# One row of the up weights in two transfers, and the order of the four matmuls that use it

## The chip, the cores and the metric

The kernel runs on one core of one Trainium2 chip. The metric is device time in microseconds (us): the median of several runs, beside the time of one profiled execution whose trace is read here. The core has TensorE (PE in the profile; PEld is its loading of weights), VectorE (DVE), ScalarE (ACT), GpSimd (POOL) and SyncE (SP), which in this kernel only issues DMA transfers.

## The reference

One layer adds two branches to its input. Inputs and output are bf16.

```
xn  = layernorm(x)                                   # x: 2048 tokens x 512
dt  = exp(log_dt);  L = exp(dt * Lambda)             # 512 complex states
Bu  = xn @ (((L - 1) / Lambda)[:, None] * B).T
h_t = L * h_(t-1) + Bu_t                             # a scan over 2048 tokens
y   = 2 * Re(h @ C.T) + xn * Dskip
f   = (silu(xn @ w_gate) * (xn @ w_up)) @ w_down     # 512 -> 1376 -> 512
out = x + y + f
```

## The kernel before, in words

The 2048 tokens are four chunks (`CW` = 512 tokens) of four tiles of 128 tokens. The instructions of each engine stand in the order in which the Python code emits them; the framework adds the semaphores. Dependences on DMA are kept by transfer: whoever reads a part of a tile waits for the transfers that wrote this part. Hardware-issued transfers take eight landing counters in turn, and an issue whose counter is still taken waits until the transfer eight places before it has landed.

Most of the span is a long sequence of matmuls, chunk after chunk: `bproj_tile` (L387, states of the scan), `gateup_tile` (L462, gate and up products), `out_ffn` (L605) and `out_ssm` (L618, the two parts of the output). VectorE's scans and rotations come between these from a backlog with planned costs (`queue`, `pump`, `need`); the coefficients `CF` of the last matmuls are made there too (L373).

The change lies at the start, where nothing is loaded yet. Chunk 0 is done token-major: a tile of tokens is the stationary side, the weights stream as the moving side, 512 columns at a time. The columns of the gate and up weights are cut into feature groups 0 and 1 (512 columns each) and a rest of 352 (`fgroups`, L89). `wg01` and `wu01` hold groups 0 and 1 of gate and up, 1024 columns (`FE`) in four rows `k`; row `k` has the weights for input features 128k to 128k + 127.

The SP queue issues, in this order: token tile 0 (L123); the four rows of up (L128, through `load_row`, L117), 256 KB each; rows 0 and 1 of gate; token tile 2 (L131); row 2 of gate; token tile 3 (L133); row 3 of gate; the rest columns of gate and up (`w_end`, L113); the tokens of chunk 1 (L141). ScalarE issues token tile 1 (L125), GpSimd three small parameter rows (L140). Later on the SP queue stand transposing transfers: chunk 0's tokens (L258) and the two parts of B (`BT`, L145), which wait for VectorE's work on tiles 2 and 3.

For tiles 0 and 1, TensorE transposes the raw tokens (L231), VectorE subtracts the mean (`centered`, L248, into `CF`, whose memory serves as scratch here) in six steps: tile 0 rows 0 and 1, tile 1 rows 0 and 1, then rows 2 and 3 of each tile in one. TensorE then multiplies row by row, `row_mm(which, k)`, with `which` 0 for up and 1 for gate: for each row four matmuls (L494), two tiles times two feature groups, into four accumulators in PSUM that are complete after row 3. ScalarE takes the up accumulators out (L514), while TensorE goes on with the gate rows, a small transpose of the parameters (L278) and the transposes of token tile 2.

Of the kernel before, what the change touches and what calls it, by code (L numbers as in the profile page):

```python
# [23 lines left out]
def kernel(  # L24
# [17 lines left out]
    nc = tc.nc  # L42
# [31 lines left out]
    def bank(shape=(128, CW), dtype=F32):  # L74
        return psum.tile(list(shape), dtype, name="ps")
# [7 lines left out]
    wu_v = B_w_up.rearrange("(k p) f -> p k f", p=128)  # L83
# [6 lines left out]
    FE = fgroups[-1][0] * 128  # L90
    wg01 = const.tile([128, KD, FE], BF16, name="wg01")
    wu01 = const.tile([128, KD, FE], BF16, name="wu01")
# [23 lines left out]
    def load_row(q, t, view, k):  # L116
        q.dma_start(out=t[:, k, :], in_=view[:, k, 0:FE])  # L117
# [7 lines left out]
    nc.scalar.dma_start(out=xall[:, 1, :], in_=x_v[:, 1, :])  # L125
    nc.scalar.preload_act_table_set("silu_and_others")
    for k in range(KD):
        load_row(nc.sync, wu01, wu_v, k)  # L128
    for k in range(HK):
        load_row(nc.sync, wg01, wg_v, k)  # L130
    nc.sync.dma_start(out=xall[:, 2, :], in_=x_v[:, 2, :])  # L131
# [93 lines left out]
    pair = [[[bank() for _ in range(2)] for _ in range(2)] for _ in range(2)]  # L225
# [260 lines left out]
    def tokens(i, k):  # L486
        if i < SW:
            return xcT[:, k, i * 128:(i + 1) * 128]
        return xnT0[:, k, i, :]

    def sw_mm(ps, groups, gi, i, k0=0, k1=KD):
        a, b = fgroups[gi]
        for k in range(k0, k1):
            nc.tensor.matmul(ps[:, 0:(b - a) * 128], lhsT=tokens(i, k), rhs=groups[gi][:, k, 0:(b - a) * 128],  # L494
                             start=(k == 0), stop=(k == KD - 1))
# [202 lines left out]
    G, U = wg_g, wu_g  # L698
# [14 lines left out]
        centered(i, HK, KD)  # L713

    def row_mm(which, k):
        for i in range(2):
            for gi in range(2):
                sw_mm(pair[which][i][gi], (U, G)[which], gi, i, k, k + 1)

    for k in range(KD):  # L720
        row_mm(0, k)
# [6 lines left out]
    for n in range(2):  # L728
        norm_dve(n)
    row_mm(1, 0)  # L730
    pp = prm_transpose()
    ln_stats(2)
# [6 lines left out]
    for k in range(1, SW):  # L739
        row_mm(1, k)  # L740
# [167 lines left out]
```

## Time and profile before

| | us |
|---|---|
| median of 3 runs | 177.86 |
| the three runs | 177.73, 177.86, 178.3 |
| the profiled execution | 178.45 |
| its span, first to last instruction | 176.2 |
| TensorE busy in the span | 171.9 (98%) |
| VectorE busy | 157.6 (89%) |
| ScalarE busy | 102.7 (58%) |
| GpSimd busy | 28.1 (16%) |

The granted TensorE clock was 1.0 throughout. The profile's rows give starts in us from the start of the span; a matmul's end is modelled, so that two matmuls that follow each other overlap in the rows. A DMA row gives the issuing engine's start and the time of the issue; the time from issue to landing stands in a separate view. "idle before" is the time in which an engine did nothing ahead of an instruction, with what ended it.

### The profile page before, as it was taken

The numbers are of one execution on the slowest core, as the hardware profiler recorded it, in microseconds if no ns is written. First come the engines' busy times: TensorE is split into PE (matmuls) and PEld (weight loads), VectorE is DVE, ScalarE is ACT, GpSimd is POOL, SyncE is SP. The second block draws the span as 40 slices with busy tenths as digits, with TensorE's granted clock in tenths as the row PEclk, the third lists the DMA queues.
The fourth block names the chain that finished last, engine by engine and source line by source line (L and its number), as shares of the span: only waits on it lengthen the run. The fifth ranks groups of instructions, "written<-read, shape, count | busy, mean of one in ns | idle before, by whom it ended". The sixth has DMA issues, their size and how long they took to land.

```text
span 176.2 us, 2377 instructions
## 1 busy us (share of the span) xinstructions
PE 171.9 (98%) x859; PEld 81.9 (46%) x859; DVE 157.6 (89%) x261; ACT 102.7 (58%) x188; POOL 28.1 (16%) x39
## 2 busy tenths in 40 slices
PE   7899999999999999999999999999999999999993
PEld 4344445464444444446444444446444444444543
DVE  3877999999999999999999999999999998699542
ACT  4179599794996685236598661024666653991100
POOL 5244110022000000044300000024100000521700
PEclk9999999999999999999999999999999999999999
DMA  5997949999999300037016000007310000696831
GB/s 169 357 342 147 142 90 208 287 188 297 151 221 309 119 0 4 0 34 85 2 30 123 0 0 0 0 0 80 43 20 12 0 0 4 93 159 106 91 87 60
DMA packets 34042, 17.87 MB, mean 101 GB/s; under 512 B 24896, under 2 KB 32928, under 8 KB 33984
## 3 DMA queue, kind: packets, MB, share of 16 engines
q1 hardware_dynamic: 30288, 14.22, 34.5%
q0 software_dynamic: 3456, 3.28, 14.6%
q10 hardware_dynamic: 288, 0.23, 0.4%
q8 instruction: 6, 0.10, 0.2%
q14 instruction: 4, 0.03, 0.1%
HBM read 8.03 MB, written 5.24 MB: 75 GB/s over the span
## 4 chain that ended last, share of the span: by engine, by line
PE 95%; DMA 3%; SPq 0%; DVE 0%; issue 0%
PE ps L462 29%; PE ps L605 22%; PE ps L618 16%; PE ps L387 16%; PE ps L494 7%; PE ps L548 3%; DMA wu<-in_B_w_up_dram 3%; PE ps L774 2%; SPq L117 0%; SPq L123 0%; DVE xall L621 0%; PE ps L231 0%; PE ps L278 0%
## 5 line engine op out<-in xcount | busy, mean ns | idle before, releaser
L605 PE MATMUL ps<-wd_sb,guT 128*128 128x512 bf16 (+4 forms) x187 | 38.9, 366 | 0.0
L429 DVE TENSOR_TENSOR_SCAN g<-r_t,car,u 128x512 bf16<-128x512 f32 x24 | 29.1, 1265 | 0.0
L618 PE MATMUL ps<-CF,wt 128*128 128x512 bf16 (+2 forms) x136 | 28.5, 366 | 0.0
L387 PE MATMUL ps<-xnT,BT 128*128 128x512 bf16 x128 | 28.3, 379 | 0.0
L605 PEld LDWEIGHTS <-guT 128*128 128x128 bf16 (+1 forms) x187 | 17.9, 98 | 20.5
L462 PE MATMUL ps<-xnT,wu 128*128 128x512 bf16 x96 | 24.6, 379 | 0.0
L462 PE MATMUL ps<-xnT,wg 128*128 128x512 bf16 x96 | 24.6, 379 | 0.0
L625 POOL DMA_DIRECT2D out_dram<-res x12 | 10.5, 1043 | 78.5 <-ACT res L624 72.5
L476 ACT ACTIVATE guT<-ps 128x512 bf16<-128x512 f32 x30 | 18.2, 606 | 4.9 <-PE ps L462 4.5
L477 ACT CAST u<-ps 128x512 bf16<-128x512 f32 x30 | 17.9, 595 | 4.8 <-PE ps L462 4.7
L389 ACT CAST u<-ps 128x512 bf16<-128x512 f32 x32 | 17.6, 594 | 4.9 <-PE ps L387 3.6
L618 PEld LDWEIGHTS <-wt 128*128 128x128 bf16 x136 | 13.0, 98 | 14.7
L387 PEld LDWEIGHTS <-BT 128*128 128x128 bf16 x128 | 12.5, 98 | 14.9
L624 ACT CAST res<-ps 128x512 bf16<-128x512 f32 x12 | 6.8, 585 | 21.4 <-PE ps L618 21.4
L579 ACT ACTIVATE xr<-xall,nb,rstd 128x512 bf16<-128x512 bf16 x16 | 11.8, 807 | 8.7 <-DVE xall L587 4.7
L462 PEld LDWEIGHTS <-wu 128*128 128x128 bf16 x96 | 9.4, 98 | 11.3
L462 PEld LDWEIGHTS <-wg 128*128 128x128 bf16 x96 | 9.3, 98 | 10.6
L192 POOL TENSOR_TENSOR rstd<-ve,neg_half 128x1 f32<-128x1 f32 (+1 forms) x7 | 7.5, 1077 | 29.4 <-DVE ve L191 28.9
L182 DVE BATCH_NORM_STATS2 stats<-xall 128x6 f32<-128x512 bf16 x16 | 10.8, 676 | 0.2 <-DMA xall<-in_A_x_dram 0.2
L462 PE MATMUL ps<-xnT,w_end 128*128 128x512 bf16 x48 | 10.8, 379 | 0.0
L481 DVE TENSOR_TENSOR guT<-guT,u 128x1024 bf16<-128x1024 bf16 x15 | 10.1, 676 | 0.0
L397 DVE TENSOR_TENSOR pm<-g,c 128x2048 bf16<-128x2048 bf16 x8 | 9.8, 1222 | 0.1
(121 smaller groups left out, 207.5 us busy)
## 6 DMA issues: line engine op xcount, KB each, us to landing
out_dram<-in_A_x_dram SPq DMA_DIRECT2D x3, 512.0 KB, 5.3
out_dram<-res POOLq DMA_DIRECT2D x12, 128.0 KB, 3.2
out_dram<-xall POOLq DMA_DIRECT2D x3, 512.0 KB, 6.7
wd_sb<-in_B_w_down_dram SPq DMA_DIRECT2D x1, 1280.0 KB, 7.9
wu<-in_B_w_up_dram SPq DMA_DIRECT2D x4, 256.0 KB, 4.6
wg<-in_B_w_gate_dram SPq DMA_DIRECT2D x4, 256.0 KB, 5.1
xall<-in_A_x_dram SPq DMA_DIRECT2D x1, 1024.0 KB, 6.9
xall<-in_A_x_dram SPq DMA_DIRECT2D x1, 512.0 KB, 6.2
```

The costliest lines, as they stand in the source:

```text
L182: nc.vector.bn_stats(out=stats[:, n, 0, :], in_=xall[:, n, :])
L387: nc.tensor.matmul(ps[:] if c else by_k(ps[:]), lhsT=BT[:, part, k, q * 128:(q + 1) * 128], rhs=xnT[:, c, k, :] if c else xnT0[:, k], star ...
L389: nc.scalar.copy(out=u_tiles[c][:, part, q, :], in_=ps[:])
L429: V.tensor_tensor_scan(out=g()[:, part, q, :], data0=r_t[:, q:q + 1].to_broadcast([128, CW]), data1=u_tiles[c][:, part, q, :], initial=ini ...
L462: nc.tensor.matmul(ps[:fs, lo:hi], lhsT=wslice(groups, fi, k), rhs=xnT[:, c, k, lo:hi], start=(k == 0), stop=(k == KD - 1))
L476: nc.scalar.activation(out=guT[:fs, fi, :], in_=psg[:fs], func=ACT.Silu)
L477: nc.scalar.copy(out=u_pair[c][:fs, fi % 2, :], in_=psu[:fs])
L494: nc.tensor.matmul(ps[:, 0:(b - a) * 128], lhsT=tokens(i, k), rhs=groups[gi][:, k, 0:(b - a) * 128], start=(k == 0), stop=(k == KD - 1))
L579: nc.scalar.activation(out=box["xr"][:], in_=xall[:, n, :], func=ACT.Identity, scale=rstd[:, n:n + 1], bias=nb[:, n:n + 1])
L605: nc.tensor.matmul(o[:], lhsT=gu_tiles[c][:fsz[fi], fi, i * 128:(i + 1) * 128], rhs=wd_sb[:fsz[fi], fi, lo:hi], start=(fi == 0), stop=False)
L618: nc.tensor.matmul(o[:], lhsT=w_tiles[c][:, part, q, i * 128:(i + 1) * 128], rhs=CF[:, part, q, lo:hi], start=False, stop=(part == 1 and q ...
L625: nc.gpsimd.dma_start(out=out_v[:, n, lo:hi], in_=res[:, lo:hi], accum_op=ALU.add)
```

## The change

The load of row 1 of `wu01` becomes two transfers of 512 columns, feature group 0 and then feature group 1, issued one after the other in the same place of the SP queue. For up row 1 alone, `row_mm` goes through the feature groups outside and the tiles inside: tile 0 and tile 1 with group 0, then tile 0 and tile 1 with group 1. The other rows, and all gate rows, keep the order tile 0 group 0, tile 0 group 1, tile 1 group 0, tile 1 group 1. The numbers of later lines move by one to three.

```diff
     for k in range(KD):
-        load_row(nc.sync, wu01, wu_v, k)
+        for lo, hi in [(0, FE // 2), (FE // 2, FE)] if k in (1,) else [(0, FE)]:
+            nc.sync.dma_start(out=wu01[:, k, lo:hi], in_=wu_v[:, k, lo:hi])
     for k in range(HK):
         load_row(nc.sync, wg01, wg_v, k)
...
     def row_mm(which, k):
-        for i in range(2):
-            for gi in range(2):
-                sw_mm(pair[which][i][gi], (U, G)[which], gi, i, k, k + 1)
+        order = [(i, gi) for i in range(2) for gi in range(2)]
+        if which == 0 and k in (1,):
+            order = [(i, gi) for gi, i in order]
+        for i, gi in order:
+            sw_mm(pair[which][i][gi], (U, G)[which], gi, i, k, k + 1)
```

## The prediction

> **What bounds the kernel now.** I read the page first, then the chain that ended last in order of time, then the timelines of TensorE, VectorE and the DMA queue in the first 24 us, with the issues and their times to landing. The page:
>
> ```profile
> span 176.2 us, 2377 instructions
> PE 171.9 (98%) x859; PEld 81.9 (46%) x859; DVE 157.6 (89%) x261; ACT 102.7 (58%) x188; POOL 28.1 (16%) x39
> ```
>
> TensorE is busy for 98% of the span, so time can only come from its few idle places or from its work, and the change leaves its 859 matmuls as they are. The chain says where the idle place is (start, us, what):
>
> ```profile
> 1.65 4.53 DMA wu<-in_B_w_up_dram
> 6.18 0.04 issue
> 6.22 3.61 PE ps L494 x16
> ...
> 22.20 0.86 PE ps L774 x4
> 23.06 6.91 PE ps L387 x32
> ...
> 73.20 6.91 PE ps L618 x32
> ...
> 173.06 0.46 PE ps L618 x8
> 173.52 0.02 issue
> 173.54 0.29 DVE xall L621
> ```
>
> From 6.22 us on, the chain is TensorE without a break, to 173.52. Before 6.22 it is a transfer of up weights, issued at 1.65, landed at 6.18, with 0.04 from landing to matmul. A microsecond won or lost at 6.22 therefore shows at the end, unless something further on that TensorE does not wait for today becomes late. Around that place (start, us, engine, line, tiles, count, idle time before and what ended it):
>
> ```profile
> 4.88 0.60 PE L494 MATMUL ps<-wu,CF 128*128 128x512 bf16 x2
> 6.22 2.75 PE L494 MATMUL ps<-wu,CF 128*128 128x512 bf16 x12 [0.73 <-DMA wu<-in_B_w_up_dram]
> 8.81 1.03 PE L494 MATMUL ps<-wg,CF 128*128 128x512 bf16 x4
> ...
> 4.01 1.67 DVE L248 TENSOR_TENSOR CF<-xnT,ps 128x128 bf16<-128x128 bf16 x6
> ```
>
> Row 0's last two matmuls start at 4.88 and one step later; the twelve of rows 1 to 3 run from 6.22 to 8.81, 0.216 us each. So TensorE could take row 1 at 4.88 + 2 x 0.216 = 5.31, and loses 0.91 us by that measure (0.73 by the modelled ends). The last row shows that the wait is the weights' alone: the six centrings end at 4.01 + 1.67 = 5.68, and row 1 needs the first four only, which come before the two wide ones. Rows 2 and 3 began at 6.22 + 4 x 0.216 = 7.08 and at 7.95, without a wait.
>
> What the transfers did: for each, its issue (start, us) and, in the same order, KB and us from issue to landing:
>
> ```profile
> 1.19 0.42 SPq L117 DMA_DIRECT2D wu<-in_B_w_up_dram  x1
> 2.13 0.43 SPq L117 DMA_DIRECT2D wu<-in_B_w_up_dram  x1
> 2.60 0.43 SPq L117 DMA_DIRECT2D wu<-in_B_w_up_dram  x1
> 3.07 0.44 SPq L117 DMA_DIRECT2D wg<-in_B_w_gate_dram  x1
> 3.56 0.43 SPq L117 DMA_DIRECT2D wg<-in_B_w_gate_dram  x1
> 4.03 0.61 SPq L131 DMA_DIRECT2D xall<-in_A_x_dram  x1
> ...
> wu<-in_B_w_up_dram SPq DMA_DIRECT2D x1, 256.0 KB, 2.9
> wu<-in_B_w_up_dram SPq DMA_DIRECT2D x1, 256.0 KB, 4.6
> wu<-in_B_w_up_dram SPq DMA_DIRECT2D x1, 256.0 KB, 4.8
> wg<-in_B_w_gate_dram SPq DMA_DIRECT2D x1, 256.0 KB, 5.2
> wg<-in_B_w_gate_dram SPq DMA_DIRECT2D x1, 256.0 KB, 5.2
> xall<-in_A_x_dram SPq DMA_DIRECT2D x1, 128.0 KB, 5.1
> ```
>
> Landings: up row 0 at 4.09, row 1 at 6.18 (chain), row 2 at 6.73, row 3 at 7.40, gate row 0 at 8.27, gate row 1 at 8.76, token tile 2 at 9.13. They come in order of issue. Row 1 comes 2.09 after row 0, while the later ones are (8.76 - 6.73)/3 = 0.68 apart: row 1 is 1.41 late by their pace, and row 2 is close behind it. That closeness decides the forecast.
>
> **The change part by part.** It removes nothing. It adds one issue on the SP queue and splits row 1's 256 KB into two landings of 128 KB; it moves two of the row's four matmuls (feature group 0 of tile 1, feature group 1 of tile 0 change places), and each pair then waits for its own half: in the built program the third matmul of the row has a wait of its own.
>
> *The added transfer in the stream.* Bytes stay the same, pieces become 1 KB. The nearest row is the token tile, 128 KB in 1 KB pieces: it lands 9.13 - 8.76 = 0.37 after its predecessor, against half of 0.68, 0.34. So a half costs 0.03 above its share, two cost 0.06; I call this delay d = 0.06. Its lower end is zero, since no byte is removed. Its upper end in ordinary running is one issue slot, 2.60 - 2.13 = 0.47, if the stream were short of issues; I do not take that, because issues are 0.47 apart and landings 0.68, so the queue is ahead of the engines. A gain below zero I exclude, as the rows behind row 1 come no earlier than their bytes.
>
> The Trainium skill, in "DMA: Bandwidth & Descriptors", section "Bandwidth", gives 0.95 us for 64 KB and 6.15 us for 1 MB, which speaks against splitting: drawn as a straight line, an estimate, 256 KB takes 1.99 and two of 128 KB take 2.60, so d would be 0.61. The row of the token tile does not bear that out, with 0.37 for 128 KB. By the page's figure row 2 would start at 7.38 and the kernel would take 178.16.
>
> *The first half.* It lands at the latest half a row's pace before the second: 6.18 + 0.06 - 0.34 = 5.90; by equal shares of the stretch from 4.09 to 6.18 at 5.14. Its pair runs at 5.31 to 5.74, or at worst 5.94 to 6.37. The second half lands at 6.24, so its pair starts at 6.28, or at worst 6.37, and row 1 ends at 6.71 to 6.81 instead of 7.08. Both ends give the same from here, because of the next step.
>
> *What is late next.* Row 2 lands at 6.73 + 0.06, its matmul starts 0.04 later: 6.83. That is after 6.81, so TensorE waits again, and row 2 starts 7.08 - 6.83 = **0.25 us** earlier, not 0.43. Row 3 is there at 7.40 + 0.06 + 0.04 = 7.50 and wanted at 7.69: no wait. Gate row 0 is there at 8.37 and wanted at 8.81 - 0.25 = 8.56: no wait; its landing would cap the gain at 8.81 - 8.37 = 0.44. Gate row 1 is there at 8.86, wanted after 9.4.
>
> *The queue behind the added issue.* Every SP issue after the first half comes up to one slot (0.47) later until an issue has to wait for an old landing. In the built program that wait is for the transfer eight back, and the places shift by one: token tile 3 now waits for the first half and gate row 3 for the second, where they waited for rows 0 and 1. The rows:
>
> ```profile
> 5.38 0.43 SPq L133 DMA_DIRECT2D xall<-in_A_x_dram  x1
> xall<-in_A_x_dram SPq DMA_DIRECT2D x1, 128.0 KB, 4.7
> 6.20 0.33 SPq L117 DMA_DIRECT2D wg<-in_B_w_gate_dram  x1
> wg<-in_B_w_gate_dram SPq DMA_DIRECT2D x1, 256.0 KB, 4.6
> ...
> 9.14 0.69 DVE L182 BATCH_NORM_STATS2 stats<-xall 128x6 f32<-128x512 bf16 x1 [0.24 <-DMA xall<-in_A_x_dram]
> 10.42 0.69 DVE L182 BATCH_NORM_STATS2 stats<-xall 128x6 f32<-128x512 bf16 x1
> 11.68 0.38 PE L494 MATMUL ps<-wg,CF 128*128 128x512 bf16 x1
> ```
>
> Gate row 3 was issued at 6.20, as row 1 landed, and will be at 6.26; it lands at 10.86 and is wanted at 11.68 - 0.25 = 11.43. Token tile 3 lands at 10.08 + 0.06, or 10.55 at worst, and VectorE takes it at 10.42. VectorE does wait for tile 2 (0.24 ahead of 9.14), so its chain moves by d, and with it the transposed loads that follow it on the SP queue. The tightest of them:
>
> ```profile
> 15.35 3.92 SPq L145 DMA_TRANSPOSE BT<-in_A_B_re_dram  x1
> BT<-in_A_B_re_dram SPq DMA_TRANSPOSE x1, 6.8
> 22.69 3.33 PEld L387 LDWEIGHTS <-BT 128*128 128x128 bf16 x16
> 67.34 5.38 DVE L373 SCALAR_TENSOR_TENSOR CF<-CT,nc2im,cm 128x512 bf16<-128x512 bf16 x8
> ```
>
> BT is there at 22.15 + 0.06 = 22.21 (22.34 if tile 3 is at its worst) and wanted at 22.69 - 0.25 = 22.44: the cover holds by 0.1 to 0.2; without it, each 0.1 of delay costs 0.1. Later the nearest cover is VectorE's last coefficient, done at 72.72, against the matmuls that start to use them at 73.20: 0.48 of room, 0.23 after the gain.
>
> *The matmuls' order.* Cost zero: four weight loads stand there before and after, and the weights of tile 1 for row 1 are the fourth narrow centring, done by 5.68 minus the two wide ones; at the earliest they are now wanted at 5.31 + 0.22 = 5.53. If it were late by all of that, 5.68, row 2's landing would still hide it.
>
> Sum: -0.25 us. The profiled execution took 178.45 (its span 176.2, 2.25 around it) and would take 178.20; it stands 0.59 above the median of the runs, 177.86, and I carry the difference over: **177.6 us**, 0.14% less. About 0.3%, 0.53 us, is what a measurement of this kernel can tell from no change, so this counts as no change.
>
> **The rivals.**
>
> *The whole wait goes (faster).* The 1.41 of lateness is a fault of this stretch and not of the bytes; with other pieces it may fall on other engines, or be shorter, and rows 2 and on then come earlier too. For it: all later spacings are 0.68, and by these row 1 would have been there at 4.77. Against: nothing in the change takes away what else runs there. The gain lies between the 0.53 that counts and the whole 0.91; halfway, 0.72: 177.14.
>
> *The lateness is one per transfer (slower).* Place: the stream between row 0 and row 2. If the 1.41 belongs to a transfer and not to the stretch, the second half brings one of its own, and rows 2, 3 and the gate rows land later by d. Row 2 starts at 6.77 + d, so it decides from d = 0.31; over 0.53 us are lost from d = 0.84. Between one issue slot, 0.47, and 1.41 the middle is 0.94: row 2 starts at 7.71, 0.63 later, 178.49. For it: one transfer did take that long. Against: the four of its size behind it did not.
>
> *The first half lands no earlier than the row did (no gain).* Both halves at about 6.24, as the slowest engine serves both late: four matmuls from 6.28, row 2 at 7.14, +0.06: 177.92. It needs a half to pass in no time, against the 0.37 of the token tile.
>
> **How the numbers follow.** The forecast has 0.46, the whole wait gone 0.22, the slower rival 0.18, the rival of no gain 0.14. Faster by over 0.3% is 0.22, slower by over 0.3% is 0.18, and within are the other two, 0.60. The range takes in the middle of both outer rivals: from 177.0, just short of the whole 0.91, to 178.5; only the far tails are left out. The forecast's own range, with d from 0 to 0.47 and the cap of 0.44, is 177.4 to 178.0.
>
> **What would show it.** In the changed kernel's timeline: two up matmuls between 5.3 and 6.4 with a wait before them shorter than 0.73; two more at about 6.3; a new short wait for a transfer of wu before row 2, at 6.8; the first gate matmul at about 8.56 instead of 8.81; the first BT matmuls 0.25 earlier and no wait for BT. I am wrong if row 2's start is not later than row 1's last matmul, if row 2 lands past 7.1, or if the gate matmuls are early and the chain after 22 us is not.

## The result, and the profile after

The changed kernel took 179.03 us (median of 6 runs, 178.79 to 179.4) and the kernel before, beside it, 177.94 (6 runs): ratio **1.0063, 95% interval 1.0042 to 1.0085**, 1.1 us slower. Forecast were 177.6 us and no change. Measured twice more, it gave 1.0021 [1.0000, 1.0041] and 1.0037 [1.0014, 1.0059]: slower by 0.4 to 1.1 us over the three, the second with an interval that reaches 1. Three single executions of the study, 1.5% or more above the fastest of their kernel, are left out of all ratios and means.

The page after:

```profile
span 176.6 us, 2378 instructions
PE 172.0 (97%) x859; PEld 82.1 (46%) x859; DVE 157.6 (89%) x261; ACT 101.4 (57%) x188; POOL 28.6 (16%) x39
```

The span has grown by 0.4 us, from 176.2. The chain that ended last (start, us, what):

```profile
2.60 4.43 DMA wu<-in_B_w_up_dram
7.03 0.04 issue
7.07 2.75 PE ps L495 x12
...
22.19 0.86 PE ps L777 x4
23.05 6.91 PE ps L388 x32
...
173.04 0.46 PE ps L619 x8
173.51 0.03 issue
173.53 0.29 DVE xall L622
```

It is the same chain, but the transfer at its head is now row 2, not row 1. From there TensorE runs without a break as before, and it reaches every later piece at the same time as before within 0.02 us: row 2 at 7.07 (7.08), the last VectorE instruction at 173.53 (173.54). In this pair of traces the start has neither gained nor lost, and the 0.4 us lie *behind* the last instruction. TensorE in the first microseconds (start, us, count, idle before and what ended it):

```profile
4.27 2.12 PE L495 MATMUL ps<-wu,CF 128*128 128x512 bf16 x8
7.07 1.89 PE L495 MATMUL ps<-wu,CF 128*128 128x512 bf16 x8 [0.68 <-DMA wu<-in_B_w_up_dram]
8.79 1.03 PE L495 MATMUL ps<-wg,CF 128*128 128x512 bf16 x4
```

The wait before row 1 is gone, rows 0 and 1 run in one piece, and 0.68 us of waiting stand before row 2 instead of 0.73 before row 1. The transfers, issue (start, us) and then, in the same order, KB and us to landing:

```profile
1.65 0.43 SPq L129 DMA_DIRECT2D wu<-in_B_w_up_dram  x1
2.12 0.43 SPq L129 DMA_DIRECT2D wu<-in_B_w_up_dram  x1
2.60 0.45 SPq L129 DMA_DIRECT2D wu<-in_B_w_up_dram  x1
3.09 0.44 SPq L129 DMA_DIRECT2D wu<-in_B_w_up_dram  x1
4.53 0.43 SPq L132 DMA_DIRECT2D xall<-in_A_x_dram  x1
...
wu<-in_B_w_up_dram SPq DMA_DIRECT2D x1, 128.0 KB, 3.6
wu<-in_B_w_up_dram SPq DMA_DIRECT2D x1, 128.0 KB, 3.6
wu<-in_B_w_up_dram SPq DMA_DIRECT2D x1, 256.0 KB, 4.4
wu<-in_B_w_up_dram SPq DMA_DIRECT2D x1, 256.0 KB, 4.6
xall<-in_A_x_dram SPq DMA_DIRECT2D x1, 128.0 KB, 5.0
```

The halves land at about 5.3 and 5.7, the first within its forecast (5.14 to 5.90), the second earlier than forecast (6.24). Row 2 lands at 2.60 + 4.43 = 7.03 (first line of the chain) and token tile 2 just before 9.52, both later than forecast (6.79 and 9.19). VectorE waits for that tile for 0.69 us instead of 0.24:

```profile
9.52 0.69 DVE L183 BATCH_NORM_STATS2 stats<-xall 128x6 f32<-128x512 bf16 x1 [0.69 <-DMA xall<-in_A_x_dram]
```

What grew at the end shows in the waits of the SP queue in the last microseconds, of the kernel before and then of the changed one (engine, line, what it waited for: us in total, times, longest):

```profile
SPq L903 <- DMA out_dram<-xall: 0.5, 1, 0.5
```

```profile
SPq L906 <- DMA out_dram<-xall: 1.0, 1, 1.0
```

SyncE ends the kernel by looking at the eight landing counters in turn, the first to the eighth. The last store was issued at 173.86 in the kernel before and at 173.85 in the changed one, and it lands at 175.30 and 175.28. In the kernel before it holds the eighth counter: the seven other looks are done by then, and after its landing come only 0.9 us of closing steps, which both kernels have. The added transfer has moved every later one on by a place, and the last store now holds the first counter: SyncE waits there for 1.0 us, and its seven further looks, 0.06 us each, come behind the landing.

### The profile page after: what moved, and what is told of

It reads as the page before. It is cut to its first block, busy times and chain, and to the rows that moved or that the text cites. A ratio compares the mean times of both kernels' runs of the same rounds, so it can differ in the third digit from the quotient of the medians.

```text
span 176.6 us, 2378 instructions
## 1 busy us (share of the span) xinstructions
PE 172.0 (97%) x859; PEld 82.1 (46%) x859; DVE 157.6 (89%) x261; ACT 101.4 (57%) x188; POOL 28.6 (16%) x39
## 4 chain that ended last, share of the span: by engine, by line
PE 94%; DMA 3%; SPq 1%; issue 0%; DVE 0%
PE ps L463 29%; PE ps L606 22%; PE ps L619 16%; PE ps L388 16%; PE ps L495 7%; PE ps L549 3%; DMA wu<-in_B_w_up_dram 3%; PE ps L777 2%; SPq L129 1%; SPq L123 0%; DVE xall L622 0%; PE ps L232 0%; PE ps L279 0%
```

## The experiments

Two numbers are read from each. The *tail* runs from the end of VectorE's last instruction to the end of the span: 2.38 us before, 2.80 after. The *mean span* over the timed runs of a measurement, taken against the mean span of the runs of the kernel before beside them on the same chip, has a standard error of 0.1 to 0.2 us for 10 to 12 runs, less than the times have.

**The end.** The changed kernel with one late transfer less (a copy of x into the output; these are issued after 50 us), so that the last store has the eighth counter again:

```diff
-    for a in range(0, (NCH - 1) * CW, CW):
-        nc.sync.dma_start(out=out[0, a:a + CW, :], in_=A_x[0, a:a + CW, :])
+    for a, b in ((0, 2 * CW), (2 * CW, 3 * CW)):
+        nc.sync.dma_start(out=out[0, a:b, :], in_=A_x[0, a:b, :])
```

> The changed kernel, with the three late copies of x to the output made two (1024 rows and 512 rows), so that the last transfer of the kernel gets the same landing counter as before. Theory of the end (the split shifts the turn of the eight counters, the last transfer gets the first one, which the end of the kernel looks at first, and seven looks of 0.06 us follow its landing): the tail from the last VectorE instruction to the end of the span falls from 2.77 to 2.35 us, and the ratio to before falls from 1.0063 to about 1.004. Theory of the start (the added transfer makes the rows behind it late, the end does not matter): ratio stays 1.006.

> The changed kernel with the old end, a second time. Theory that the end is the whole loss: mean span within 0.15 us of the kernel before, ratio 0.999 to 1.001. Theory that the start loses too: mean span 0.25 us or more over it, ratio above 1.0015.

Measured: tail 2.39 and 2.40 us; ratios 1.0024 [1.0001, 1.0047] and 1.0000 [0.9983, 1.0017]; mean span +0.24 and +0.11. With the old end the changed kernel loses little, at the edge of what can be told from noise. The complement, the kernel before with four late copies instead of three, so that only the end changes:

```diff
+    for a, b in ((0, CW // 2), (CW // 2, CW), (CW, 2 * CW), (2 * CW, 3 * CW)):
```

> The kernel before, with the three late copies of x to the output made four, at about 60 us: nothing changes in the first 25 us, but the turn of the landing counters shifts by one as in the changed kernel. Theory of the end: 0.41 us slower, ratio 1.0023, tail 2.77 us. Theory of the start: ratio 1.000.

> The kernel before with the changed kernel's end and the old start, a second time. Both theories: mean span 0.4 us over the kernel before, ratio 1.002 to 1.003. If the theory that the end is the whole loss holds, the changed kernel is the same as this one within 0.15 us.

Measured: tail 2.83 and 2.81; ratios 1.0037 [1.0012, 1.0062] and 1.0016 [1.0000, 1.0031]; mean span +0.59 and +0.33. The kernel with the old start and the new end is slower, as the changed one is; beside the second of these measurements the changed kernel's mean span was a further 0.33 higher, so that the end was not the whole loss there. The SP queue of the kernel with four copies ends with the changed kernel's wait:

```profile
SPq L903 <- DMA out_dram<-xall: 1.0, 1, 1.0
```

Two single executions show whether it is the counter's place that counts, with the same copies made two or five in the kernel before:

> The kernel before, with the late copies of x to the output made two: the last transfer takes the seventh of the eight landing counters instead of the eighth. Theory of the end: one look of 0.06 us is left behind the landing, tail from the last VectorE instruction 2.44 us (2.38 before, 2.80 in the changed kernel). If the tail depended on something else than the counter's place, 2.38 or anything else.

> The kernel before, with the late copies made five: the last transfer takes the second counter. Theory of the end: six looks are left behind its landing, tail 2.74 to 2.77 us. Against it: 2.38 us, or 2.80 us as for the first counter if any shift costs the same.

Measured: 2.46 us with the seventh counter, 2.76 with the second. The four places make one line:

```
counter of the last store    first        second  seventh  eighth
looks behind its landing     7            6       1        0
tail, us                     2.80 - 2.83  2.76    2.46     2.38 - 2.40
traces                       5            1       1        13
```

This part is settled: 0.06 us for each place that the last store stands ahead of the eighth, 0.42 us for the change.

**The start, the split and the order of the matmuls.** The split with the old order of the four matmuls, with two copies:

> Row 1 in two transfers, but the four matmuls in the old order, so that the second one already needs the second half; two copies, so that the end is as before. Theory of the start: same time as with the new order within 0.1%, since TensorE waits for row 2 in any case, about 1.004 to 1.006. If the new order of matmuls itself cost something, this one would be faster than the split with the new order.

Measured: 1.0023 [1.0007, 1.0039], mean span +0.28, as with the new order. The order costs and gains nothing that shows; in the trace with the old order TensorE waits 0.41 us for row 2 too. The three measurements with the split and the old end average +0.21 us, with a standard error of about 0.1: the start loses about 0.2, where a gain of 0.25 was forecast. That is little more than noise, since the kernel before without its parameter loads, below, gave +0.16 with row 1 as late as ever.

One execution did what the forecast said, the second one with two copies. There, as in the trace of before, TensorE ran at full speed from 3.90 us on; row 2 starts at 6.82 (forecast 6.83), the first gate matmul at 8.55 (8.56), and the span is 176.0 with the old end:

```profile
4.28 1.15 PE L495 MATMUL ps<-wu,CF 128*128 128x512 bf16 x4
5.85 2.86 PE L495 MATMUL ps<-wu,CF 128*128 128x512 bf16 x12 [0.42 <-DMA wu<-in_B_w_up_dram]
8.55 0.81 PE L495 MATMUL ps<-wg,CF 128*128 128x512 bf16 x3
```

Row 2's first matmul, among the twelve of the second line:

```profile
6.82 0.59 PE L495 MATMUL ps<-wu,CF 128*128 128x512 bf16 x2
```

In the other five traces with row 1 alone split on SP, row 2 starts at 7.07 to 8.53; in the seven traces with the old start, at 6.60 to 7.51. The start differs more from execution to execution than the change was to move it.

All four up rows split, with seven copies for the old end:

```diff
-        for lo, hi in [(0, FE // 2), (FE // 2, FE)] if k in (1,) else [(0, FE)]:
+        for lo, hi in [(0, FE // 2), (FE // 2, FE)] if k in (0, 1, 2, 3) else [(0, FE)]:
...
-        if which == 0 and k in (1,):
+        if which == 0:
```

> All four up rows in two transfers each, all with the matmuls by feature group, and seven late copies so that the end is as before. Theory of the start as on record (each half costs 0.03 us in the stream): the four further added transfers put the gate rows and what follows 0.2 to 0.3 us later, but TensorE can use each half as it lands, so that its last wait is for a half of row 2 or 3: span 0.1 to 0.3 us shorter than with row 1 alone split (about 176.4), ratio 0.999 to 1.002. Rival (an added issue or transfer costs the stream some tenths, as it would by a transfer of its own weight): span 177 or more, ratio above 1.004.

Measured: 1.0058 [1.0037, 1.0080], mean span +0.76. The rival in the expectation holds by its ratio (its span of 177 or more did not quite come, with 176.8). The second halves of rows 1 and 2, the first gate row and token tile 2:

```profile
2.60 0.47 SPq L129 DMA_DIRECT2D wu<-in_B_w_up_dram  x1
3.59 0.43 SPq L129 DMA_DIRECT2D wu<-in_B_w_up_dram  x1
5.01 0.43 SPq L117 DMA_DIRECT2D wg<-in_B_w_gate_dram  x1
5.97 0.43 SPq L132 DMA_DIRECT2D xall<-in_A_x_dram  x1
...
wu<-in_B_w_up_dram SPq DMA_DIRECT2D x1, 128.0 KB, 3.1
wu<-in_B_w_up_dram SPq DMA_DIRECT2D x1, 128.0 KB, 3.4
wg<-in_B_w_gate_dram SPq DMA_DIRECT2D x1, 256.0 KB, 4.3
xall<-in_A_x_dram SPq DMA_DIRECT2D x1, 128.0 KB, 4.4
```

These two halves land 3.1 and 3.4 us behind the start of their issue, where the whole rows of the kernel before took ever longer (4.5, 4.6, 4.8). A half takes 0.47 us to issue, and in the kernel before the stream took 0.34 for as many bytes; so a stream of halves can go no faster than its issues, and on the middle one of the DMA engines the second to the eighth half land 0.46 us apart, as they are issued. TensorE's wait is now before the first gate row, which it starts at 9.40 instead of 8.81:

```profile
9.40 0.82 PE L495 MATMUL ps<-wg,CF 128*128 128x512 bf16 x3 [0.61 <-DMA wg<-in_B_w_gate_dram]
```

VectorE takes token tile 2 at 10.35 instead of 9.14, 1.2 us late for four added issues.

**The slot of the queue, or the split.** Issue and pieces were taken apart: a small load that nobody reads in the kernel before (two copies, as above); and the split with the second half issued by ScalarE (two copies):

```diff
     for k in range(KD):
         load_row(nc.sync, wu01, wu_v, k)
+        if k == 1:
+            nc.sync.dma_start(out=scratch[:], in_=x_v[:, 0, 0:32])
```

```diff
-    nc.scalar.preload_act_table_set("silu_and_others")
     for k in range(KD):
         for lo, hi in [(0, FE // 2), (FE // 2, FE)] if k in (1,) else [(0, FE)]:
-            nc.sync.dma_start(out=wu01[:, k, lo:hi], in_=wu_v[:, k, lo:hi])
+            (nc.scalar if lo else nc.sync).dma_start(out=wu01[:, k, lo:hi], in_=wu_v[:, k, lo:hi])
+    nc.scalar.preload_act_table_set("silu_and_others")
```

> The kernel before with one small added transfer (128 partitions of 32 columns of x, 8 KB, read by nobody) issued on the SP queue between up rows 1 and 2, and two late copies so that the end is as before. Nothing is split. Theory of the slot (what an added issue costs the rows behind it is the 0.47 us of the SP queue, because the engines work the first rows off almost as fast as they are issued): the landing of row 3 on the middle of the sixteen engines moves from 6.25 to 6.52 us in the six traces without an added issue to 6.7 to 7.3 us, as in the three traces with the split (6.93 to 7.29); ratio 1.001 to 1.003. Rival (the cost lies in the split transfer's smaller pieces): row 3 stays at 6.3 to 6.5 us.

> The small added load between rows 1 and 2 on the SP queue, a second time. Theory that an added slot costs the start about 0.2 us: mean span 0.1 to 0.3 us over the kernel before; its first result (0.26 us under it) was then chance. If it is under it again, an added slot by itself costs nothing, and the loss at the start belongs to the split on the SP queue.

> Row 1 split and the new order of matmuls, but the second half is issued by ScalarE behind token tile 1 (ahead of its table load), so that the SP queue has no added issue; two late copies, so that the end is as before. Theory of the slot: row 3 lands on the middle engine at 6.2 to 6.5 us as without the split, token tile 2 lands no later than in the kernel before (9.1 to 9.6 us), and the ratio is 0.998 to 1.001. Rival of the pieces: row 3 at 6.9 us or later, ratio 1.002 or more. Row 0 may land up to 0.3 us later, since the half now competes with it.

> The version with the second half issued by ScalarE and the old end, a second time, as the candidate that beats both kernels (0.9977 before, the interval to 1.0006). If it does, mean span 0.2 to 0.4 us under the kernel before and ratio 0.998 again; if the first result was chance, 1.000.

And a slot taken away: row 1 whole, issued by ScalarE (`load_row(nc.scalar if k == 1 else nc.sync, ...)`, the table load behind it).

> The kernel before, nothing split, with up row 1 issued by ScalarE behind token tile 1 instead of by SP: rows 2, 3 and all behind are issued 0.47 us earlier. Theory of the slot: row 3 lands on the middle engine 0.2 to 0.5 us earlier than before (about 6.0 us), the last wait of TensorE ends earlier or is gone, ratio 0.997 to 0.999. Rival (the stream is bound by the engines alone, not by the issues): row 3 at 6.3 to 6.5 us and ratio 1.000; slower, if row 0 comes so much later that TensorE's first row waits.

> Up row 1 whole, issued by ScalarE, a second time. If the split is what gains in the version with the half on ScalarE (mean span 0.29 us under the kernel before over two submissions), this one, which has no split, stays within 0.15 us of the kernel before. If taking work off the SP queue is what gains, it is 0.2 to 0.4 us under it again (0.30 the first time).

The middle landing below is the mean of the eighth and ninth of the sixteen engines' landings in the trace, which leaves the slowest engine out (TensorE waits for the slowest):

```
                                     row 3, middle landing, us            ratio                 mean span, us
not split, 7 traces                  6.25 - 6.52                          1                      0
small load on SP, 2                  6.67, 6.75                           0.9984, 1.0016        -0.26, +0.07
half on ScalarE, 2                   6.54, 6.35                           0.9977, 0.9988        -0.31, -0.38
row 1 on ScalarE, 2                  6.59, 6.26                           0.9978, 0.9996        -0.31, -0.02
split on SP, 6                       6.93, 7.15, 7.29, 6.90, 7.23, 7.04   1.0000 to 1.0024      +0.24, +0.11, +0.28
                                                                          (old end)
```

The intervals: small load [0.9961, 1.0007] and [0.9995, 1.0037]; half on ScalarE [0.9949, 1.0006] and [0.9967, 1.0010]; row 1 on ScalarE [0.9959, 0.9998] and [0.9968, 1.0024]. The split on the SP queue makes row 3 some 0.7 us late on the middle engine. The slot alone makes it 0.3 late and costs no time that shows; the split alone, with the half issued elsewhere, hardly moves it. Taking a slot away does not bring row 3 forward, so in the kernel before it is not the issues that set the pace, as the prediction read it; the theory of the slot in its simple form falls with this. What is shown is that neither the slot nor the split loses by itself what the two lose together. One thing was not kept apart: ScalarE issues the half at 1.30, SP at 2.12, so the version on ScalarE may also gain by the earlier issue.

Why the two together lose is open. That the halves leave the engines without work for part of each slot is a natural guess, but the profile does not show it. From 4 to 7 us (the stretch and its length; busy time of PE, PEld, DVE, ACT and POOL with their instructions; granted clock, busy share of the DMA engines, GB/s), the kernel before, the changed kernel, the small load, and the half on ScalarE the second time:

```profile
4.00:7.00 3.00, 2.15 (x13) 0.80 (x11) 2.88 (x10) 0.78 (x3) 0.22 (x1) 1.00 0.97 323
```

```profile
4.00:7.00 3.00, 2.40 (x12) 0.90 (x10) 2.87 (x10) 0.71 (x3) 0.28 (x1) 1.00 0.99 276
```

```profile
4.00:7.00 3.00, 2.14 (x13) 0.78 (x11) 2.85 (x10) 0.81 (x3) 0.19 (x1) 1.00 0.97 296
```

```profile
4.00:7.00 3.00, 3.00 (x13) 1.15 (x11) 2.85 (x10) 0.80 (x3) 0.20 (x1) 1.00 0.99 329
```

The six traces with the split on SP move 240 to 276 GB/s there, the seven with the old start 305 to 350, at the same busy share: by this view the engines are as busy as before and move fewer bytes.

The Trainium skill, "DMA: Bandwidth & Descriptors", section "Issuing engines are not separate DMA queues", says that issuing on several engines saves only the sequencer's issue time, which is usually small beside the transfer. Here the issue took 0.43 us for 128 KB, and moving one issue to ScalarE turned +0.2 us into -0.3. The version with the half on ScalarE is the fastest here by its spans, 0.31 and 0.38 us under the kernel before; its ratios lie below 1 both times, each with an interval that reaches 1. Its two traces do not show where the gain lies: TensorE waits for no row in them, but full speed came late (6.94 and 6.41 us). How much of the gain is the split's is not settled, since row 1 whole on ScalarE was under the kernel before in one of its two measurements.

**The lateness of row 1.** The kernel before, without GpSimd's parameter loads:

```diff
-    nc.gpsimd.memset(prm_rows[:], 0.0)
-    for i, v in enumerate((A_Lambda_re, A_Lambda_im, A_log_dt)):
-        nc.gpsimd.dma_start(out=prm_rows[i * NQ:(i + 1) * NQ, :], in_=v.rearrange("(q j) -> q j", j=128))
+    nc.gpsimd.memset(prm_rows[:], -0.5)
```

> The kernel before without GpSimd's three small parameter loads: the parameter rows hold a constant instead, so the scan's parameters are other numbers. The loads' packets are what runs on the DMA engines besides the weights from 4.1 us to 7.7 us. Theory that they make row 1's slowest engines late: row 1 lands near 5.0 us, TensorE's wait before row 1 is gone or under 0.2 us, and the span falls by 0.5 to 0.9 us (ratio 0.995 to 0.997). Theory that the lateness comes from the weights' own stream: row 1 lands at 5.3 to 6.6 us as in the other traces, ratio 1.000.

Measured: 1.0022 [1.0003, 1.0042], mean span +0.16 (a slowdown that nothing in its trace explains), and row 1 as late as ever:

```profile
6.11 2.75 PE L492 MATMUL ps<-wu,CF 128*128 128x512 bf16 x12 [0.43 <-DMA wu<-in_B_w_up_dram]
```

These loads are not what makes it late. What does was not found.

**The kernels again.** 

> The kernel before, unchanged, as a second look at its start and as a measure of noise. Both theories: ratio 1.000 within 0.3%. In its trace, row 1's landing shows how much of the first profile's 2.09 us after row 0 belongs to that one execution: if the wait of TensorE before row 1 is again 0.6 to 0.8 us, the first trace was typical; if it is under 0.4 us, the first trace overstated what there was to gain.

> The changed kernel once more, on the same chip as the other three. If the two causes add, the late stream (about 0.3 us by the spans of the two kernels with the split and the old end) and the end (0.42 us), its ratio is 1.004 to 1.006; a ratio near 1.002 would mean that one of the two does not count.

> The changed kernel a third time, beside the same with the old end. Theory that the end is the whole loss: ratio 1.002 to 1.004, mean span 0.42 us over that of the kernel before. Theory that the start loses as much again: mean span 0.7 us or more over it.

The kernel before against itself gave 1.0010 [0.9995, 1.0025], mean span +0.09, with waits of 0.54 us before row 1 and 0.21 before row 2. The changed kernel's mean span was +0.36 and +0.67, 0.51 on average; the end's 0.42 and the start's 0.2 make 0.6, which agrees within the errors. The first comparison's 1.1 us is more than that: there the kernel before stood at 177.94 in 6 runs, in the five later measurements at 178.13 to 178.50. The changed kernel's mean span was much the same then and later (176.77, then 176.73 and 176.90). The last half microsecond of the first comparison is not explained by any trace.

## Why the prediction was wrong

**The wait moves to row 2: right.** The mechanism was the one forecast, with the wait in the forecast place. The first rival, the whole wait gone, did not come; nor did the rival in which the first half lands no earlier, since the halves landed at about 5.3 and 5.7. In one execution of six even the size came out, with row 2 at 6.82.

**The step "the added transfer in the stream": wrong in size.** It put d at 0.06 us from the token tile's landing behind its predecessor, and excluded an issue slot, since issues were 0.47 apart and landings 0.68. Row 2 landed at 7.03, 0.30 later than before (6.73); VectorE took tile 2 at 9.52, 0.38 later. On the middle engine row 3 is 0.7 late. The 0.68 were distances between the slowest engines' landings, and the 0.06 came from a transfer further down the queue. With d = 0.30, row 2 starts at 6.77 + 0.30 = 7.07 by the prediction's own rule, as was seen; its break-even was d = 0.31. The 0.61 that the prediction worked out from the Trainium skill and set aside was nearer than 0.06 for the middle engine, though the split with its halves on two queues did not show that cost. Why a half cost this much is open, as said above. The slower rival was thus right in its place and its break-even, but not in its price: d went past 0.84 in one of the six traces with row 1 alone split on SP (row 2 at 8.53), and by the mean spans the start lost 0.2 us, not 0.63.

**The step "the queue behind the added issue": incomplete, and the larger part of the loss that the traces explain.** It noted that the places of the eight counters shift by one, followed the shift for the waits of tile 3 and gate row 3, where it cost nothing, and did not follow it to the end of the kernel, where 0.42 us were lost in every trace with the last store on the first counter. No rival had it. The trace of before showed the wait of 0.5 us at the end; what the place of the last counter was worth could have been read from the order of the looks there.

**The start was read from one execution.** In the trace of before TensorE ran at full speed from 3.90 us on; over the twenty traces of the study the clock's records begin, at full speed, between 3.90 and 6.94 us. (The granted clock of 1.0 that the views give does not tell this; they give 1.00 from 4 to 6 us of the trace below too.) Where it comes late, rows 0 and 1 run at 0.43 us a matmul and eat up the wait. An example is the first trace of the split with two copies, where eight matmuls took 2.96 us instead of 1.9, with a late row 2 behind them:

```profile
4.37 2.96 PE L495 MATMUL ps<-wu,CF 128*128 128x512 bf16 x8
8.53 1.89 PE L495 MATMUL ps<-wu,CF 128*128 128x512 bf16 x8 [1.19 <-DMA wu<-in_B_w_up_dram]
```

The Trainium skill, "TensorE: Matmul & The Clock Gate", section "Part 1: The HAM clock gate (the "warmup" mystery)", says that full clock comes after a window of some 3.4 us of activity that runs freely and does not start with the kernel; the spread here, 3.0 us, fits within one such window, though it is more than the half microsecond either way that the section gives. In the seven traces with the old start TensorE's wait before row 1 was 0.98, 0.82, 0.73, 0.54, 0.43 and twice nothing, and the 0.73 is the one that the prediction read. So what it took as lost there was above what a run loses on average, and the gain on offer was smaller than one trace said.

**The matmuls' order and the covers: right.** The old order gave the same time. BT was there at 15.89 + 6.6 = 22.49, 0.3 later than forecast, and TensorE did not wait for it.

## What to carry to other kernels

An added transfer can cost in three places: in the stream of bytes, in the issue slot of its queue, and in everything that goes by the number of transfers; follow each to the last instruction of the kernel. Splitting the transfer that is waited for helps by no more than the distance to the next landing; look first at what lands behind it, and on the slowest engine. Read a stall at the start of a kernel from several executions before pricing it.

## What was not expected of the hardware

GpSimd's second power of four columns per partition (`r_t`) took 1.01 us in some executions and 1.54 in others, with the same operands; the kernel before and then the changed one (start, us, duration):

```profile
13.40 1.01 POOL L285 TENSOR_TENSOR r_t<-e_t,dre 128x4 f32<-128x4 f32 x1 [0.28 <-DVE ws L290]
13.66 0.69 DVE L529 TENSOR_TENSOR guT<-guT,u 128x1024 bf16<-128x1024 bf16 x1 [0.20 <-ACT guT L502]
```

```profile
13.78 1.54 POOL L286 TENSOR_TENSOR r_t<-e_t,dre 128x4 f32<-128x4 f32 x1 [0.27 <-DVE ws L291]
13.76 0.69 DVE L530 TENSOR_TENSOR guT<-guT,u 128x1024 bf16<-128x1024 bf16 x1
```

All seven traces with a split on the SP queue have the long form, but so have three others, and row 1 on ScalarE had it once and once not. What separates them is the order: in all ten long cases VectorE's product into `guT` started 0.02 us before `r_t`, in all ten short ones 0.05 to 0.78 us after it. So GpSimd's instruction takes about 0.5 us longer when VectorE's has started first; no run set this order on purpose. GpSimd's next work (`jidx`) comes later by as much, and VectorE waits for it for 1.86 us instead of 1.05; TensorE did not wait for it in the changed kernel.
